# Top-k attention followed by an MLP: four units before the weight rounding, chunks from 128 tokens on, and one transpose for the leftover keys of both tiles

## The chip, the cores and the metric

The kernel runs on one core of a Trainium2 chip. The metric is device time in microseconds (us) of one execution, and the median over several executions is compared. Five engines with a queue of instructions each work side by side: TensorE (PE in the profile; its weight loads are PEld), VectorE (DVE), ScalarE (ACT), GpSimd (POOL) and SyncE (SP), which here only issues DMAs. Every engine takes its own instructions in the order in which the program issued them, and waits on semaphores for the others.

## The reference

Attention in which every query keeps its 32 best keys, for 8 batches of 8 heads with 576 tokens and 64 features per head, and then a two-layer MLP with a leaky ReLU on the 4608 tokens of 512 features (8 heads times 64):

```
scores = q @ k.T / sqrt(64)                     # per batch and head: 576 x 576
kth    = 32nd largest score of each row
scores = where(scores >= kth, scores, -1e9)
attn   = exp(scores - max) ; attn /= sum(attn) + 1e-9
x      = attn @ v                               # bridged to 4608 x 512
h      = x @ w_in                               # 512 x 2048
out    = max(0.01 * h, h) @ w_out               # 2048 x 512
```

The two weight matrices arrive as float64, everything else as float32; all matmuls run in float32.

## The kernel before, in words

**Units.** Heads are handled in pairs: 32 pairs, four per batch (HP = 4), and a pair's queries and keys lie in one 128-partition tile, head 0 on partitions 0 to 63, head 1 on 64 to 127. A *unit* is 256 rows of scores, held as two tiles of 128 rows x 576 keys (`u.s[0]`, `u.s[1]`). A whole unit is 128 queries of one pair, one head per tile. 576 = 4 x 128 + 64, so 64 queries per head are left over; a left unit takes these 64 queries of two pairs. There are 18 units per batch (16 whole, 2 left) and 144 in all. In even batches (`first`, line 161) the left units come first, in odd ones last, so that the left units of two neighbouring batches meet.

**Stages of a unit.** `scores` (L168): TensorE, and two ScalarE copies (L184) to SBUF. `top_k` (L187): VectorE, four rounds of "eight largest" (L194) on both tiles, with the eight found values struck out in between (L197). `mask` (L202): GpSimd, two passes per tile (L208, L210). `exponents` and `sums` (L212, L216): ScalarE. `reciprocals` (L220): one small VectorE instruction. `normalize` (L224): ScalarE. Then the normalized weights are transposed on TensorE with an identity as moving operand: the 576 keys are cut into five pieces (KLEN, L47), four of 115 keys and one of 116. `transpose_main` (L227) transposes the four pieces of one tile and copies them out (L234); `transpose_tail` (L236) transposes the fifth piece of each tile, two transposes, and copies both out (L240). `weigh_values` (L254) multiplies with the values (L262), ten matmuls per pair of heads, and ScalarE copies the result to the x tile of its chunk (L272).

**MLP.** The 4608 tokens are cut into chunks (CHUNKS, L51): 64, 128, 128, sixteen of 256 and one of 192. When all units of a chunk are through `weigh_values`, its MLP (`mlp`, L274) may start. It is a generator: 16 blocks of the first layer (L282, four matmuls each, then a leaky ReLU on ScalarE, L288) and, per 128 tokens, 16 matmuls of the second layer (L294). The chip executes each float32 matmul of these as two instructions, so a chunk has 128 instructions on L282 and 32 on L294 for each 128 tokens or part of them.

**Order of work.** Everything is issued by hand in steps (L397). In step s VectorE works on `top_k` of unit s, GpSimd on the mask of unit s-1, ScalarE on the exponents of unit s-2, and unit s-3 (LAG = 3, `oldest`) is normalized, transposed and weighed; `scores` of unit s+2 is issued near the end of the step, after `weigh_values`. In seven places (SLOTS) of a step `mlp_steps` issues a share of the MLP work that is ready, so that a chunk's MLP is spread evenly up to the step in which the next chunk becomes ready (`slot_budget`, L354). The last chunk's MLP comes after the loop (L446).

**Weight rounding.** The float64 weights come in 16 pieces of 1 MB, into three buffers (`raws`). `convert_weights` (L104) rounds a piece to float32: two VectorE passes (L112, L113), four ScalarE passes (L115 to L118), three more VectorE passes (L120 to L124). `convert` (L370) finishes the piece that was started two calls earlier, starts a new one, and issues the load of a later one. In the kernel before, units 0 and 1 (left units of batch 0) stand in steps 0 and 1; steps 2, 3 and 4 have no unit, and in each of them six calls of `convert` are issued (ROUNDED, L333), 18 calls for 16 pieces. Steps 5 on have units 2 on. Chunk 0 is ready after step 4, chunk 1 after step 11, chunk 2 after step 15, chunk 3 after step 23, and then a chunk every eight steps.

**Start.** The queries and keys of pairs 0 to 3, the scores of units 0 and 1 and the first weight pieces are issued ahead of the loop (L382 to L389).

Of the kernel before, what the change touches and what calls it, by code (L numbers as in the profile page):

```python
# [8 lines left out]
F32 = mybir.dt.float32  # L9
# [2 lines left out]
ALU = mybir.AluOpType  # L12

NKC = 5
KSTEP = 115


@with_exitstack
def kernel(
# [6 lines left out]
    moe_w_out: bass.AP,  # L26
    out: bass.AP,
):

    nc = tc.nc
    NPAIR, P, S = qT.shape
    D = P // 2
# [8 lines left out]
    HS = S // 2  # L43
    NFC = DFF // P
    ROUNDS = TOPK // 8
    WCH = 1024
    KLEN = [KSTEP] * (NKC - 1) + [S - (NKC - 1) * KSTEP]  # L47
    KMAX = KLEN[-1]
    LEFT = S % P
    assert D == 64 and S == 576 and HP == 4 and B % 2 == 0 and LEFT == 64  # L50
    CHUNKS = [64, 128, 128] + [256] * 16 + [192]  # L51
    assert sum(CHUNKS) == B * S
    CHMAX = max(CHUNKS)
    LOADED, LOADED_V = 6, 5
# [3 lines left out]
    loads = ctx.enter_context(tc.tile_pool(name="loads", bufs=LOADED))  # L58
    raws = ctx.enter_context(tc.tile_pool(name="raws", bufs=3))
    work = ctx.enter_context(tc.tile_pool(name="work", bufs=2))  # L60
    small = ctx.enter_context(tc.tile_pool(name="small", bufs=5))
    ps_sc = ctx.enter_context(tc.tile_pool(name="ps_sc", bufs=1, space=bass.MemoryType.PSUM))
    ps_tr = ctx.enter_context(tc.tile_pool(name="ps_tr", bufs=2, space=bass.MemoryType.PSUM))
    ps_ml = ctx.enter_context(tc.tile_pool(name="ps_ml", bufs=2, space=bass.MemoryType.PSUM))

    ident = const.tile([P, P], F32, name="ident")
# [61 lines left out]
    qk_of, v_of = {}, {}  # L128
# [6 lines left out]
        qk_of[pi] = qt, kt  # L135

    def load_v(pi):
        v_of[pi] = loads.tile([KMAX, NKC, 2, D], F32, name="vt", bufs=LOADED_V)
        nc.sync.dma_start(v_of[pi], vk[pi])

    class Unit:
# [3 lines left out]
        def __init__(self, b, pairs, q0):  # L145
            self.b, self.q0 = b, q0
            if len(pairs) == 1:
                self.rows = P
                self.parts = [(0, pairs[0], 0, 0), (1, pairs[0], 1, 0)]
                self.outs = [(pairs[0], 0, 1)]  # L150
            else:
                self.rows = LEFT

                self.parts = [(0, pairs[0], 0, 0), (1, pairs[0], 1, LEFT),
                              (1, pairs[1], 0, 0), (0, pairs[1], 1, LEFT)]
                self.outs = [(pairs[0], 0, 1), (pairs[1], 1, 0)]
            self.pairs = pairs

    units = []
    for b in range(B):  # L160
        first = b % 2 == 0
        whole = [Unit(b, [b * HP + hp], q0 + LEFT * first)
                 for q0 in range(0, S - LEFT, P) for hp in range(HP)]
        left = [Unit(b, [b * HP + hp, b * HP + hp + 1], 0 if first else S - LEFT)
                for hp in range(0, HP, 2)]
        units += left + whole if first else whole + left

    def scores(u):  # L168
        ps = [ps_sc.tile([P, 2, 512], F32, name=f"psc{i}") for i in range(2)]
        for n in range(0, len(u.parts), 2):  # L170
            for half in range(2):
                for i, pi, side, r0 in u.parts[n:n + 2]:
                    qt, kt = qk_of[pi]
                    d = slice(side * D, (side + 1) * D)
                    nc.tensor.matmul(  # L175
                        ps[i][r0:r0 + u.rows, half, 0:HS],
                        qt[d, u.q0:u.q0 + u.rows],
                        kt[d, half * HS:(half + 1) * HS],
                        start=True, stop=True,
                    )  # L180
        u.s = []
        for i in range(2):
            s_sb = work.tile([P, S], F32, name=f"s_sb{i}", bufs=5)
            nc.scalar.copy(s_sb.rearrange("p (h n) -> p h n", h=2), ps[i][:, :, 0:HS])  # L184
            u.s.append(s_sb)

    def top_k(u):  # L187

# [37 lines left out]

    def transpose_main(u, i):  # L227
        if i == 0:
            u.wT = work.tile([KMAX, 2, NKC, P], F32, name="wT")
        main = ps_tr.tile([P, 4, P], F32, name="main", tag="tr")  # L230
        for c in range(NKC - 1):
            nc.tensor.transpose(main[0:KLEN[c], c, :],  # L232
                                u.s[i][:, c * KSTEP:c * KSTEP + KLEN[c]], ident)
        nc.scalar.copy(u.wT[0:KSTEP, i, 0:NKC - 1, :], main[0:KSTEP])  # L234

    def transpose_tail(u):  # L236
        tail = ps_tr.tile([P, 2, P], F32, name="tail", tag="tr")
        for i in range(2):
            nc.tensor.transpose(tail[0:KMAX, i, :], u.s[i][:, (NKC - 1) * KSTEP:S], ident)  # L239
        nc.scalar.copy(u.wT[:, :, NKC - 1, :], tail[0:KMAX])  # L240

# [2 lines left out]
    def x_at(token):  # L246

        c = 0
        while token >= CHUNKS[c]:
            token -= CHUNKS[c]  # L250
            c += 1
        return c, token

    def weigh_values(u):  # L254
        n = u.rows
        po = ps_tr.tile([P, len(u.outs), n], F32, name="po", tag="tr")
        for o, (pi, i0, i1) in enumerate(u.outs):
            vt = v_of[pi]
            for c in range(NKC):
                for side, i in ((0, i0), (1, i1)):  # L260
                    r0 = LEFT * side if n < P else 0
                    nc.tensor.matmul(  # L262
                        po[side * D:(side + 1) * D, o, :],
                        vt[0:KLEN[c], c, side, :],
                        u.wT[0:KLEN[c], i, c, r0:r0 + n],
                        start=(c == 0), stop=(c == NKC - 1),
                    )
        ch, col = x_at(u.b * S + u.q0)
        if ch not in x_of:
            x_of[ch] = [xpool.tile([P, CHMAX], F32, name=f"x{c}") for c in range(HP)]  # L270
        for o, (pi, _, _) in enumerate(u.outs):
            nc.scalar.copy(x_of[ch][pi % HP][:, col:col + n], po[:, o, :])  # L272

    def mlp(ch):  # L274

        n = CHUNKS[ch]
        t0 = sum(CHUNKS[:ch])
# [32 lines left out]
    backlog, owed = [0.0], [0.0]  # L310
# [18 lines left out]
    LAG = 3  # L329


    steps = units[:2] + [None] * 3 + units[2:]
    ROUNDED = {2: 6, 3: 6, 4: 6}  # L333

    def unit(n):
        return steps[n] if 0 <= n < len(steps) else None
# [2 lines left out]
    for n, u in enumerate(steps):  # L339
        if u is None:  # L340
            continue
        ch, _ = x_at(u.b * S + u.q0)
# [11 lines left out]
    def slot_budget(s):  # L354

        after = [at for at, _ in ready_at if at >= s]
        return backlog[0] / ((after[0] + 1 - s if after else 1) * SLOTS)

    SLOTS = 7
    converting = []  # L360
# [3 lines left out]
    def fetch_weights():  # L364
        chunk = next(chunks, None)
        got = load_weights(*chunk) if chunk else None
        if got:
            raw_chunks.append(got)
# [11 lines left out]
    with tc.manual_schedule():  # L380
        last = {p: n for n, u in enumerate(steps) if u for p in u.pairs}
        for p in range(HP):  # L382
            load_qk(p)
            if p % 2:
                scores(units[p // 2])
                fetch_weights()
        for p in range(HP):
            load_v(p)
        fetch_weights()  # L389

        def load_more(s):

            for of, load, n, lag in ((qk_of, load_qk, LOADED, -2), (v_of, load_v, LOADED_V, LAG)):
                while len(of) < NPAIR and (len(of) < n or last[len(of) - n] + lag <= s):
                    load(len(of))

        for s in range(len(steps) + LAG):  # L397
            cur, old = unit(s), unit(s - 1)
            older, oldest, new = unit(s - 2), unit(s - LAG), unit(s + 2)
            picks = top_k(cur) if cur else iter(())  # L400
            budget = slot_budget(s)
            rounded = ROUNDED.get(s, 0)

            def slot(n):
                next(picks, None)
                for _ in range(rounded * n // 3 - rounded * (n - 1) // 3 if n else 0):
                    convert()

            slot(0)
            if old:  # L410
                mask(old, 0)
                mask(old, 1)
            if oldest:
                normalize(oldest, 0)
                normalize(oldest, 1)
            mlp_steps(budget)
            if older:
                exponents(older, 0)
            if oldest:
                transpose_main(oldest, 0)  # L420
            mlp_steps(budget)
            if older:
                exponents(older, 1)
                sums(older)
            slot(1)
            if oldest:
                transpose_main(oldest, 1)
            mlp_steps(budget)
            if oldest:
                transpose_tail(oldest)  # L430
            slot(2)
            mlp_steps(budget)
            if older:
                reciprocals(older)
            mlp_steps(budget)
            slot(3)
            if oldest:
                weigh_values(oldest)
            if new:
                scores(new)  # L440
            mlp_steps(budget)
            mlp_steps(budget)
            attended(s)
            if s >= max(ROUNDED):
                load_more(s)
        mlp_steps(1e9)  # L446

# [44 lines left out]
```

## Time and profile before

| | us |
|---|---|
| median of 3 runs (lowest to highest) | 1714.21 (1713.75 to 1714.6) |
| the profiled execution's own time | 1713.03 |
| its span in the profile | 1710.9 |
| TensorE busy (matmuls) | 1598.3 |
| VectorE busy | 1488.2 |
| GpSimd busy | 1079.5 |
| ScalarE busy | 1033.8 |

Busy time is the time in which an engine executes something; share and time alone do not say what a stage waits for. The chain that ended last is followed back from the last instruction and tells which engine's work stood in line. The span is shown in 40 slices of 42.8 us, with the busy share of each engine and the granted TensorE clock in tenths. "PE busy" counts matmuls that overlap in the pipeline; what a matmul costs in line is read from the distance between starts in the chain, not from the mean of one. L numbers are lines of the kernel before.

### The profile page before, as it was taken

The numbers are of one execution on the slowest core, as the hardware profiler recorded it, in microseconds if no ns is written. First come the engines' busy times: TensorE is split into PE (matmuls) and PEld (weight loads), VectorE is DVE, ScalarE is ACT, GpSimd is POOL, SyncE is SP. The second block draws the span as 40 slices with busy tenths as digits, with TensorE's granted clock in tenths as the row PEclk, the third lists the DMA queues.
The fourth block names the chain that finished last, engine by engine and source line by source line (L and its number), as shares of the span: only waits on it lengthen the run. The fifth ranks groups of instructions, "written<-read, shape, count | busy, mean of one in ns | idle before, by whom it ended". The sixth has DMA issues, their size and how long they took to land.

```text
span 1710.9 us, 26732 instructions
## 1 busy us (share of the span) xinstructions
PE 1598.3 (93%) x9664; PEld 1097.1 (64%) x9664; DVE 1488.2 (87%) x3106; ACT 1033.8 (60%) x2310; POOL 1079.5 (63%) x726
## 2 busy tenths in 40 slices
PE   1158998999999999999999999999999999999999
PEld 0146665858585858585758585858585858585764
DVE  7999999999899999999899999999899999999600
ACT  3965666656565656565656565656565656565530
POOL 4007777776667676767676767676667676767600
PEclk7557999999999999999999999999999999999999
DMA  5530010000110010000110010000100010000000
GB/s 181 197 133 1 5 62 23 14 7 9 61 35 7 7 62 28 14 8 7 63 35 7 7 62 28 14 7 7 63 35 7 7 35 28 7 7 7 7 13 10
DMA packets 21715, 56.30 MB, mean 33 GB/s; under 512 B 2000, under 2 KB 2000, under 8 KB 20560
## 3 DMA queue, kind: packets, MB, share of 16 engines
q1 hardware_dynamic: 21584, 54.60, 9.2%
q8 instruction: 77, 1.26, 0.3%
q14 instruction: 54, 0.44, 0.1%
HBM read 45.15 MB, written 9.44 MB: 32 GB/s over the span
## 4 chain that ended last, share of the span: by engine, by line
PE 85%; DVE 11%; ACT 3%; DMA 0%; issue 0%; SPq 0%; ACTq 0%
PE pz L294 29%; PE ph L282 28%; PE po L262 10%; PE psc L175 9%; PE main L232 7%; DVE tops L194 5%; DVE rest L197 4%; PE tail L239 2%; DVE ex L122 1%; ACT ex L116 1%; ACT ex L115 1%; DVE w_in L124 0%; ACT ex L117 0%; ACT s_sb L225 0%; ACT raw L118 0%; DVE w_in L120 0%
## 5 line engine op out<-in xcount | busy, mean ns | idle before, releaser
L208 POOL TENSOR_SCALAR pen<-s_sb,tops 128x576 f32<-128x576 f32 x288 | 638.0, 2215 | 417.7 <-ACT wT L240 214.0
L194 DVE MAX8 tops<-rest 128x8 f32<-128x576 f32 x864 | 608.1, 746 | 0.0
L282 PE MATMUL ph<-x,w_in 128*128 128x256 f32 (+3 forms) x2560 | 574.8, 369 | 4.3 <-ACT x L272 4.1
L294 PE MATMUL pz<-w_out,gT 128*128 128x512 f32 (+1 forms) x1184 | 553.7, 599 | 0.0
L282 PEld LDWEIGHTS ph<-x,w_in 128*128 128x128 f32 x2560 | 446.1, 196 | 82.8 <-issue 38.9
L197 DVE MATCH_REPLACE8 rest<-tops,rest 128x576 f32<-128x576 f32 x576 | 423.5, 743 | 0.0
L210 POOL TENSOR_TENSOR s_sb<-s_sb,pen 128x576 f32<-128x576 f32 x288 | 407.3, 1414 | 24.1
L294 PEld LDWEIGHTS pz<-w_out,gT 128*128 128x128 f32 (+1 forms) x1184 | 204.4, 187 | 203.5 <-issue 201.1
L232 PEld LDWEIGHTS main<-ident,s_sb 128*115 128x115 f32 x1152 | 165.3, 182 | 159.8 <-issue 92.2
L184 ACT COPY s_sb<-psc 128x576 f32<-128x576 f32 x288 | 170.0, 642 | 153.2 <-PE psc L175 153.2
L232 PE MATMUL main<-ident,s_sb 128*115 128x128 f32 x1152 | 177.8, 278 | 78.0 <-ACT s_sb L225 77.9
L213 ACT ACTIVATE s_sb<-s_sb,nbias 128x576 f32<-128x576 f32 x288 | 222.7, 773 | 10.9 <-POOL s_sb L210 10.9
L262 PEld LDWEIGHTS po<-wT,vt 115*64 115x64 f32 (+1 forms) x3200 | 160.0, 139 | 94.7 <-issue 73.8
L225 ACT ACTIVATE s_sb<-s_sb,rz 128x576 f32<-128x576 f32 x288 | 207.1, 770 | 9.9 <-DVE rz L222 9.7
L197 DVE MATCH_REPLACE8 rest<-tops,s_sb 128x576 f32<-128x576 f32 x288 | 211.7, 743 | 0.0
L262 PE MATMUL po<-wT,vt 115*64 115x128 f32 (+3 forms) x3200 | 193.6, 269 | 18.8 <-ACT wT L234 18.3
L194 DVE MAX8 tops<-s_sb 128x8 f32<-128x576 f32 x288 | 202.0, 743 | 9.5 <-ACT s_sb L184 9.5
L175 PE MATMUL psc<-kt,qt 64*128 64x288 f32 (+1 forms) x1280 | 202.5, 440 | 7.1 <-DMA kt<-in_kT_dram 7.1
L234 ACT COPY wT<-main 115x512 f32<-115x512 f32 x288 | 165.6, 575 | 58.5 <-PE main L232 58.3
L288 ACT ACTIVATE gT<-ph 128x256 f32<-128x256 f32 (+3 forms) x320 | 115.9, 363 | 135.8 <-PE ph L282 134.9
L272 ACT COPY x<-po 128x128 f32<-128x128 f32 (+1 forms) x160 | 39.3, 256 | 231.3 <-PE po L262 231.3
L175 PEld LDWEIGHTS psc<-kt,qt 64*128 64x128 f32 (+1 forms) x1280 | 108.7, 181 | 56.0 <-issue 23.4
(31 smaller groups left out, 535.3 us busy)
## 6 DMA issues: line engine op xcount, KB each, us to landing
vt<-in_vk_dram SPq DMA_DIRECT2D x32, 290.0 KB
qt<-in_qT_dram SPq DMA_DIRECT2D x32, 288.0 KB
kt<-in_kT_dram SPq DMA_DIRECT2D x32, 288.0 KB
out_dram<-o_sb SPq DMA_DIRECT2D x35, 256.0 KB
raw<-in_moe_w_in_dram SPq DMA_DIRECT2D x8, 1024.0 KB
raw<-in_moe_w_out_dram SPq DMA_DIRECT2D x8, 1024.0 KB
out_dram<-o_sb SPq DMA_DIRECT2D x2, 128.0 KB
```

What stands on the lines that cost most here:

```text
L175: nc.tensor.matmul(ps[i][r0:r0 + u.rows, half, 0:HS], qt[d, u.q0:u.q0 + u.rows], kt[d, half * HS:(half + 1) * HS], start=True, stop=True,)
L184: nc.scalar.copy(s_sb.rearrange("p (h n) -> p h n", h=2), ps[i][:, :, 0:HS])
L194: nc.vector.max(out=u.tops[:, i, r, :], in_=src[i])
L197: nc.vector.match_replace(out=rest[i], in_to_replace=u.tops[:, i, r, :], in_values=src[i], imm_value=LOWEST)
L208: nc.gpsimd.tensor_scalar(pen, u.s[i], u.tops[:, i, ROUNDS - 1, 7:8], MASKED, ALU.is_lt, ALU.mult)
L210: nc.gpsimd.tensor_tensor(u.s[i], u.s[i], pen, ALU.add)
L213: nc.scalar.activation(u.s[i], u.s[i], AF.Exp, bias=u.nbias[:, i:i + 1], scale=SCALE, accum_out=u.z[:, i:i + 1])
L225: nc.scalar.activation(u.s[i], u.s[i], AF.Copy, bias=0.0, scale=u.rz[:, i:i + 1])
L232: nc.tensor.transpose(main[0:KLEN[c], c, :], u.s[i][:, c * KSTEP:c * KSTEP + KLEN[c]], ident)
L262: nc.tensor.matmul(po[side * D:(side + 1) * D, o, :], vt[0:KLEN[c], c, side, :], u.wT[0:KLEN[c], i, c, r0:r0 + n], start=(c == 0), stop=(c ...
L282: nc.tensor.matmul(ph[:, 0:n], w_in[c][:, f * P:(f + 1) * P], x[c][:, 0:n], start=(c == 0), stop=(c == HP - 1),)
L294: nc.tensor.matmul(pz[0:m, 0:DMODEL], gT[f][:, r0:r0 + m], w_out[f // 4][:, f % 4, :], start=(f == 0), stop=(f == NFC - 1),)
```

## The change

Four things are changed together.

1. **Start and rounding.** The order of left and whole units is swapped between even and odd batches, so that batch 0 begins with whole units. Units 0 to 3 stand in steps 0 to 3. Steps 4 to 9 have no unit (`GAP = 6`), and in each of them three calls of `convert` are issued, 18 as before. Units 4 on stand in steps 10 on. In the steps without a unit, `scores` of a coming unit is issued at the start of the step instead of the end.
2. **Chunks.** 128, 128, then seventeen of 256. Units 0 to 3 are the first chunk; it is ready after step 6, and `slot_budget` spreads its MLP over steps 7 to 9. The second chunk (units at steps 10 to 13) is ready after step 16, the third after step 24, then one every eight steps. The chunk after the loop has 256 tokens instead of 192.
3. **Keys in pieces of 128.** The keys of head 1 are rotated by 64 places on the host. Four pieces of 128 keys per tile are transposed as before; head 0's 64 leftover keys are the last 64 columns of tile 0, and head 1's the first 64 columns of tile 1. The two score tiles become halves of one tile (`u.both`), so that these 128 columns lie side by side, and one transpose takes them both. The tail is one transpose and a copy of 128x128 instead of two and a copy of 116x256. The values are laid out by the host to match, with zeros for the other head's leftover keys.
4. **Left units** take head 0 in tile 0 and head 1 in tile 1 for both pairs.

```diff
-    CHUNKS = [64, 128, 128] + [256] * 16 + [192]
+    CHUNKS = [128] * 2 + [256] * 17
...
-        v_of[pi] = loads.tile([KMAX, NKC, 2, D], F32, name="vt", bufs=LOADED_V)
+        v_of[pi] = loads.tile([P, NKC, 2, D], F32, name="vt", bufs=LOADED_V)
...
-                self.outs = [(pairs[0], 0, 1)]
+                self.outs = [(pairs[0], 0, 0)]
...
-                              (1, pairs[1], 0, 0), (0, pairs[1], 1, LEFT)]
-                self.outs = [(pairs[0], 0, 1), (pairs[1], 1, 0)]
+                              (0, pairs[1], 0, LEFT), (1, pairs[1], 1, 0)]
+                self.outs = [(pairs[0], 0, LEFT), (pairs[1], LEFT, 0)]
...
-        first = b % 2 == 0
+        first = b % 2 == 1
...
-        u.s = []
+        u.both = work.tile([P, 2, S], F32, name="s_sb", bufs=5)
+        u.s = [u.both[:, i, :] for i in range(2)]
         for i in range(2):
-            s_sb = work.tile([P, S], F32, name=f"s_sb{i}", bufs=5)
-            nc.scalar.copy(s_sb.rearrange("p (h n) -> p h n", h=2), ps[i][:, :, 0:HS])
-            u.s.append(s_sb)
+            nc.scalar.copy(u.s[i].rearrange("p (h n) -> p h n", h=2), ps[i][:, :, 0:HS])
...
-            u.wT = work.tile([KMAX, 2, NKC, P], F32, name="wT")
+            u.wT = work.tile([P, 2 * (NKC - 1) + 1, P], F32, name="wT")
         main = ps_tr.tile([P, 4, P], F32, name="main", tag="tr")
         for c in range(NKC - 1):
-            nc.tensor.transpose(main[0:KLEN[c], c, :],
-                                u.s[i][:, c * KSTEP:c * KSTEP + KLEN[c]], ident)
-        nc.scalar.copy(u.wT[0:KSTEP, i, 0:NKC - 1, :], main[0:KSTEP])
+            k0 = c * P + i * (S - (NKC - 1) * P)
+            nc.tensor.transpose(main[:, c, :], u.s[i][:, k0:k0 + P], ident)
+        nc.scalar.copy(u.wT[:, i * (NKC - 1):(i + 1) * (NKC - 1), :], main)
 
     def transpose_tail(u):
-        tail = ps_tr.tile([P, 2, P], F32, name="tail", tag="tr")
-        for i in range(2):
-            nc.tensor.transpose(tail[0:KMAX, i, :], u.s[i][:, (NKC - 1) * KSTEP:S], ident)
-        nc.scalar.copy(u.wT[:, :, NKC - 1, :], tail[0:KMAX])
+        tail = ps_tr.tile([P, P], F32, name="tail", tag="tr")
+        both = u.both.rearrange("p i n -> p (i n)")
+        nc.tensor.transpose(tail, both[:, (NKC - 1) * P:NKC * P], ident)
+        nc.scalar.copy(u.wT[:, 2 * (NKC - 1), :], tail)
...
-                        vt[0:KLEN[c], c, side, :],
-                        u.wT[0:KLEN[c], i, c, r0:r0 + n],
+                        vt[:, c, side, :],
+                        u.wT[:, c + side * (NKC - 1) if c + 1 < NKC else 2 * (NKC - 1), r:r + n],
...
-    steps = units[:2] + [None] * 3 + units[2:]
-    ROUNDED = {2: 6, 3: 6, 4: 6}
+    FIRST, GAP = 4, 6
+    steps = units[:FIRST] + [None] * GAP + units[FIRST:]
+    gap = range(FIRST, FIRST + GAP)
...
         after = [at for at, _ in ready_at if at >= s]
-        return backlog[0] / ((after[0] + 1 - s if after else 1) * SLOTS)
+        until = gap[-1] if s in gap else after[0] if after else s
+        return backlog[0] / ((until + 1 - s) * SLOTS)
...
             load_qk(p)
-            if p % 2:
-                scores(units[p // 2])
-                fetch_weights()
+            if p < 2:
+                scores(units[p])
+        for _ in range(3):
+            fetch_weights()
         for p in range(HP):
             load_v(p)
-        fetch_weights()
...
-                for _ in range(rounded * n // 3 - rounded * (n - 1) // 3 if n else 0):
+                if s in gap and n:
                     convert()
 
             slot(0)
+            if new and s in gap:
+                scores(new)
...
-            if new:
+            if new and s not in gap:
                 scores(new)
...
-            if s >= max(ROUNDED):
+            if s >= gap[-1]:
                 load_more(s)
```

More of the change, by code (lines that the diff above doesn't have):

```diff
@@ L14 @@
 NKC = 5
-KSTEP = 115
 @with_exitstack
@@ L46 @@
     WCH = 1024
-    KLEN = [KSTEP] * (NKC - 1) + [S - (NKC - 1) * KSTEP]
-    KMAX = KLEN[-1]
     LEFT = S % P
     assert D == 64 and S == 576 and HP == 4 and B % 2 == 0 and LEFT == 64
-    CHUNKS = [64, 128, 128] + [256] * 16 + [192]
+    CHUNKS = [128] * 2 + [256] * 17
     assert sum(CHUNKS) == B * S
@@ L256, in weigh_values @@
         po = ps_tr.tile([P, len(u.outs), n], F32, name="po", tag="tr")
-        for o, (pi, i0, i1) in enumerate(u.outs):
+        for o, (pi, r0, r1) in enumerate(u.outs):
             vt = v_of[pi]
             for c in range(NKC):
-                for side, i in ((0, i0), (1, i1)):
-                    r0 = LEFT * side if n < P else 0
+                for side, r in ((0, r0), (1, r1)):
                     nc.tensor.matmul(
                         po[side * D:(side + 1) * D, o, :],
-                        vt[0:KLEN[c], c, side, :],
-                        u.wT[0:KLEN[c], i, c, r0:r0 + n],
+                        vt[:, c, side, :],
+                        u.wT[:, c + side * (NKC - 1) if c + 1 < NKC else 2 * (NKC - 1), r:r + n],
                         start=(c == 0), stop=(c == NKC - 1),
@@ L401 @@
             budget = slot_budget(s)
-            rounded = ROUNDED.get(s, 0)
             def slot(n):
                 next(picks, None)
-                for _ in range(rounded * n // 3 - rounded * (n - 1) // 3 if n else 0):
+                if s in gap and n:
                     convert()
             slot(0)
+            if new and s in gap:
+                scores(new)
             if old:
@@ L461, in by_pair, with keys_of_head_1_rotated @@
         return a.reshape(b * h // 2, 2, s, d).transpose(0, 1, 3, 2).reshape(b * h // 2, 2 * d, s)
+    def keys_of_head_1_rotated(a):
+        half = a.shape[1] // 2
+        return _np.concatenate([a[:, :half], _np.roll(a[:, half:], a.shape[2] % 128, axis=2)], axis=1)
     def by_key(a):
         b, h, s, d = a.shape
-        last = s - (NKC - 1) * KSTEP
-        keys = _np.arange(NKC)[None, :] * KSTEP + _np.arange(last)[:, None]
-        return a.reshape(b * h // 2, 2, s, d)[:, :, keys, :].transpose(0, 2, 3, 1, 4)
+        pairs, full, left = b * h // 2, s // 128, s % 128
+        a = a.reshape(pairs, 2, s, d)
+        laid = _np.zeros((pairs, 128, full + 1, 2, d), a.dtype)
+        laid[:, :, :full] = a[:, :, :full * 128].reshape(pairs, 2, full, 128, d).transpose(0, 3, 2, 1, 4)
+        for side in range(2):
+            laid[:, side * left:(side + 1) * left, full, side] = a[:, side, full * 128:]
+        return laid
     def bits(a):
@@ L473 @@
         "qT": by_pair(inputs["q"]),
-        "kT": by_pair(inputs["k"]),
+        "kT": keys_of_head_1_rotated(by_pair(inputs["k"])),
         "vk": by_key(inputs["v"]),
```

## The prediction

> **What bounds the kernel now.** I read the page first: engines, slices, chain by engine.
>
> ```profile
> PE 1598.3 (93%) x9664; PEld 1097.1 (64%) x9664; DVE 1488.2 (87%) x3106; ACT 1033.8 (60%) x2310; POOL 1079.5 (63%) x726
> ...
> PE   1158998999999999999999999999999999999999
> ...
> DVE  7999999999899999999899999999899999999600
> ...
> PEclk7557999999999999999999999999999999999999
> ...
> PE 85%; DVE 11%; ACT 3%; DMA 0%; issue 0%; SPq 0%; ACTq 0%
> ```
>
> TensorE is the chain from about slice 4 to the end; before that it idles at half clock and VectorE (later ScalarE) leads. So there are two sums: when the TensorE stretch begins, and how much TensorE work is left then. Next, the chain in order of time over the start:
>
> ```profile
> 10.40 1.41 DVE tops L194 x2
> ...
> 29.78 0.83 DVE ex L112
> ...
> 86.61 1.16 ACT ex L115
> ...
> 87.79 1.16 ACT ex L116
> ...
> 88.97 1.06 ACT ex L117
> 90.03 1.03 ACT raw L118
> ...
> 112.99 1.23 DVE w_out L120
> ...
> 116.60 1.32 DVE tops L194 x2
> ```
>
> Units 0 and 1 take 10.40 to 29.78, 9.69 us each. The rounding takes 86.8 us (29.8 to 116.6). ScalarE needs 4.38 us per weight piece (86.61 on; the neighbours 4.34 and 4.39), VectorE 4.86 (starts of L112 at 76.11 and 81.03, with a wait of 0.06): both are nearly full. After 116.6 a unit takes 9.70 us on VectorE while TensorE has little MLP; 19 steps and 2.1 us of waits later, at 302.9, step 24 brings the first 256-token MLP. From there steps take 10.6 us on TensorE:
>
> ```profile
> 571.63 0.44 PE main L232 x4
> ...
> 574.24 0.22 PE tail L239 x2
> 574.46 1.73 PE ph L282 x8
> 576.18 1.25 PE po L262 x20
> 577.43 1.17 PE psc L175 x8
> ...
> 1658.55 20.80 PE ph L282 x128
> 1679.35 27.62 PE pz L294 x64
> ```
>
> A transpose costs 0.11 us in line, a first-layer instruction of 256 columns 0.216 (1.73/8), one of 192 columns 0.1625 (20.80/128), a second-layer one 0.4315. The last two lines are the chunk after the loop. From 302.9 to the end of the span are 1408.0 us.
>
> **The change part by part.** The sum is against the profiled execution: 1713.03 us, span 1710.9; the median of 1714.21 is 1.2 above it and gets the same difference.
>
> *Start.* Unit 0 now needs pair 0 alone. Its inputs were there at 4.50 (first matmul on L175); eight instructions took 2.29 us at half clock (125.94), the copy 0.65: VectorE starts at 7.5 instead of 10.4. Four units of 9.69: rounding begins at 46.3. The swap of left and whole units costs nothing else here.
>
> *Rounding.* VectorE's work is the same 18 calls, 86.8 us if nothing else led. ScalarE gets more. Of units 1 to 3, what falls between the first and last piece: normalizations 1.33 per unit, exponents 1.75, copies of transposes 1.17, x 0.2; together 0.9 + 4.45 + 2.7. Sixteen leaky ReLUs of 128 columns (0.26 to 0.28 each): 4.2. Scores of units 4 and 5: 2 x 1.08. That is 14.4, with 16 x 4.38 = 70.1 in all 84.5; before it was 78.4 of busy time in the same stretch. ScalarE also waits for TensorE where several MLP shares lie between two pieces, since first-layer results have two buffers: two blocks at the start of step 7, scores and about three blocks between steps 7 and 8, a second-layer share and scores between 8 and 9. A block of eight 128-column instructions is 0.89 us at full clock (186.83 to 187.72) and, taken double, 1.78 at half. Counted along ScalarE's order, these waits are 6.9 us at full clock, 15.8 at half. TensorE is on and off there, so I take the middle, 11. With 0.94 ahead (first L112 to first L115), 3.6 behind (the last three VectorE passes) and 1.0 for waits on VectorE (3.9 before, when it led): 101 us, ending at 147.3. Ends: 89 (no such wait; VectorE's 86.8 lies below) and 107. That the MLP of chunk 0 itself is done by then costs nothing further: its TensorE time falls where TensorE was idle.
>
> *Steps 10 to 24.* Fifteen steps of 9.70 on VectorE: 145.5, ending at 292.8. Steps 10 to 16 have no MLP, and steps 17 to 24 spread 128 tokens over eight steps. That load is in the trace (steps 16 to 23, row 265.00), with VectorE full:
>
> ```profile
> 117.00:126.00 9.00, 9.00 (x41) 7.73 (x41) 9.00 (x20) 2.07 (x6) 0.44 (x2) 0.50 0.01 2
> 126.00:136.00 10.00, 10.00 (x45) 8.36 (x44) 10.00 (x22) 3.59 (x11) 7.83 (x6) 0.50 0.00 1
> ...
> 265.00:275.00 10.00, 7.54 (x67) 6.04 (x66) 10.00 (x22) 6.66 (x19) 7.78 (x6) 1.00 0.09 31
> ```
>
> (Windows; columns: length, busy PE, PEld, DVE, ACT, POOL, granted clock, DMA share, GB/s.) But there the clock was already full; now it will have fallen. In the rows at 117 and 126 TensorE was busy throughout and stayed at 0.50; it reached 1.00 at about 149, 4 us after transposes and MLP blocks began to alternate at 145.14. Step 17 alternates just so; 4 us at half clock lose about 2, part of it inside VectorE's cover: I take 1.5. Ends: 0, and 13 (a stretch like 117 to 140 at half clock, half of it lost).
>
> The Trainium skill, "TensorE: Matmul & The Clock Gate", Part 1, has full clock after some 3.4 us of sustained activity and half after an idle window of that length, and advises against idle gaps over 3 us, which steps 10 to 12 have. The 23 us at 0.50 disagree with the first half. By the page the loss would be 1.7 us, an estimate, and by the worse row 13.
>
> *TensorE work from there.* Before, at 302.9: 16 MLPs of 256 tokens and one of 192; 126 units to transpose and weigh, 121 to score. After, at 292.8: 17 of 256; 128 and 123. MLP: 128 x (0.216 - 0.1625) = +6.9; the second layer is the same 64 instructions per chunk, 192 or 256. Two units more: 2 x (0.88 + 1.25 + 1.17) = +6.6, less 1.8 since two fewer of the dearer left scores remain (2.09 against 1.17): +4.8. Tails: 126 x 0.22 against 128 x 0.11: -13.6. The main transposes' stationary tile grows from 115 to 128 columns: the nearest row is the first layer with 128 columns both ways, 0.111 per instruction against 0.11, +1.0. Ends: 0, and 8 x 128 x 14 ns = +14.3 if the whole difference of the mean loads (196 ns for 128 columns, 182 for 115) shows. Together -0.9. Ten weigh matmuls per pair of heads stay ten; a stationary tile of 64 columns stays 64.
>
> The same page (LDWEIGHTS) has the load grow with columns, P/1.2 ns, whatever the rows: 13 columns more are 10.8 ns, by estimate 11 us over the 1024 transposes if none is hidden. The 0.111 row speaks for hidden.
>
> *What hides the rest.* A TensorE step falls to 10.51 us; VectorE's 9.70 is next, 0.8 to spare, then GpSimd's 7.5 per unit. The smaller tail copy is off the path. SP: the values of pair 0 stand behind three weight pieces, 5.3 MB at 190 GB/s, about 28 us; they are needed near 45. A later piece's load had 7.3 us between its buffer's release (37.4) and its use (44.7) without a wait, and rounding gets slower. Later pairs are loaded from 147 instead of 117, and needed near 270.
>
> Sum: 292.8 - 302.9 = -10.1; +1.5; -0.9: -9.5. Profiled execution 1703.5, median 1704.7.
>
> **Rivals.**
> 1. Rounding stays as short as VectorE and ScalarE alone allow (89 us): 12 us less, 1692.7. For it: ScalarE waits hidden by MLP blocks done ahead during a piece. Against: two buffers.
> 2. Slower: the clock stays at half through steps 17 to 24. TensorE has 3.4 us of unit and 28.0/8 = 3.5 of MLP per step at full clock, 13.8 at half, against 9.70: 4.1 per step, 33 in all, 1736. It passes the old time from 2.7 such steps on. For it: 117 to 140 at 0.50; against: the rise at 149.
> 3. The loads of 128-column transposes show in full: +13.3, 1718, and the tail's gain is gone.
>
> **How the numbers follow.** My forecast 0.58 (of it 0.05 within 0.2%), rival 1 0.17, rival 2 0.10, rival 3 0.10 (half within 0.2%), others, such as steps above 9.70 or rounding beyond 107, 0.05, half of them slower. 0.2% (3.4 us) is about what a measurement can tell from no change. Faster 0.53 + 0.17 = 0.70; same 0.12; slower 0.18. Range 1692 (rival 1) to 1717 (the 13 us of cold clock, nearly all of rival 3); gap ends alone give 1693 to 1711. Rival 2 lies outside.
>
> **What would show it.** First L194 at 7.5; first L112 near 46, next L194 near 147 with ScalarE above 90% busy between; VectorE steps of 9.70 until 293; chain steps of 10.5; tail x1 at 0.11, main x4 still 0.44; a last chunk of 27.7 + 27.6. Wrong if the clock row reads 0.50 past step 17, if main x4 grows, or if the rounding misses 89 to 107.

## The result and the profile after

The changed kernel takes 1724.89 us (median of 4 runs, 1723.86 to 1725.7) against 1713.98 of the kernel before on the same chip: ratio 1.0065, 95% interval [1.0047, 1.0082]. It is slower by 11 us where 9.5 us less were forecast, and outside the range. The profiled execution took 1724.5 us, its span is 1722.3. Lines of the changed kernel have other numbers: L173 are the scores, L191 and L194 `top_k`, L222 `normalize`, L210 `exponents`, L230 and L236 the main and tail transposes, L258 `weigh_values`, L278 and L284 the first layer and its leaky ReLU, L290 the second layer, L113 to L116 ScalarE's part of the rounding.

The page of the changed kernel, engines, slices and chain by engine:

```profile
PE 1575.8 (91%) x9360; PEld 1057.2 (61%) x9360; DVE 1488.7 (86%) x3106; ACT 1014.5 (59%) x2293; POOL 1079.9 (63%) x726
...
PE   3255689999999999999999999999999999999999
...
PEclk9987589999999999999999999999999999999999
...
PE 80%; DVE 10%; ACT 9%; issue 0%; DMA 0%; SPq 0%; ACTq 0%
```

TensorE is busy 22 us less, as the change removes transposes and matmuls, but it is on the chain for 80% instead of 85% of the span, and ScalarE's share rose from 3% to 9%. Part of that is the rounding. The 9s with which the clock row begins are not to be taken at their word: the eight score instructions at 4.45 took 2.31 us, where eight later ones take 1.17. The chain in order of time over the start:

```profile
4.45 2.31 PE psc L173 x8
...
7.41 1.41 DVE tops L191 x2
...
43.35 1.46 DVE rest L194 x2
...
142.61 1.23 DVE w_out L118
...
146.23 1.32 DVE tops L191 x2
...
280.66 1.44 ACT s_sb L222 x2
...
291.19 0.66 PE main L230 x4
```

VectorE starts at 7.41; the last two searches of unit 3 end near 46.1; the rounding lasts to 146.23; VectorE leads until 280.5, and the first transposes of step 25, with which the first 256-token MLP begins, start at 291.19. In the kernel before they belong to step 24:

```profile
302.47 0.69 PE L232 MATMUL main<-ident,s_sb 128*115 128x128 f32 x4 [0.35 <-ACT s_sb L225]
```

So the start brought 11.3 us. They were lost afterwards: from there to the end of the span are 1431.1 us, before 1408.4. The chain in the middle of the run, over one step with first-layer work:

```profile
557.91 1.94 PE ph L278 x8
559.85 0.02 issue
559.87 0.38 ACT gT L284
560.25 0.67 ACT s_sb L222
560.92 0.04 issue
560.97 0.66 PE main L230 x4
561.63 0.86 PE ph L278 x4
562.49 0.44 PE main L230 x4
...
563.79 0.11 PE tail L236
...
568.91 1.94 PE ph L278 x8
```

The step takes 11.00 us (557.91 to 568.91), 0.38 more than before in spite of the cheaper tail. The chain leaves TensorE after eight instructions of the first layer: ScalarE applies the leaky ReLU to the block that has just ended (0.38), then normalizes tile 0 of the next unit (0.67), and only then the transposes of that tile may start. Meanwhile TensorE has one more share of MLP work, four instructions, 0.86 us; then it stands still for 0.28 us. In the kernel before, sixteen first-layer instructions stood ahead of the first transposes, and no ScalarE line was on the chain.

A step without the wait takes 10.51 us (first experiment below), so the wait costs 0.49, more than the 0.28. The timeline of another such step shows the rest. In it the transposes of tile 0 wait, those of tile 1 do not; the number in brackets is the idle time before, with what ended it:

```profile
647.08 0.42 PEld L230 LDWEIGHTS main<-ident,s_sb 128*128 128x128 f32 x4 [0.68 <-ACT s_sb L222]
647.08 0.66 PE L230 MATMUL main<-ident,s_sb 128*128 128x128 f32 x4 [0.28 <-ACT s_sb L222]
...
647.57 1.03 PE L278 MATMUL ph<-x,w_in 128*128 128x256 f32 x4
...
648.23 0.57 PEld L230 LDWEIGHTS main<-ident,s_sb 128*128 128x128 f32 x4
...
648.44 0.60 PE L230 MATMUL main<-ident,s_sb 128*128 128x128 f32 x4
...
648.88 1.03 PE L278 MATMUL ph<-x,w_in 128*128 128x256 f32 x4
```

The chain's 0.66 and 0.44 for `main` are not the same measure. After a wait the chain counts from the first start to the last end; without one it counts from the end of the matmul before, which is still running when the first transpose starts. From start to start the four transposes take 0.49 after the wait (647.08 to 647.57) and 0.44 without (648.44 to 648.88). These 0.05 us go with the first weight load, which begins together with the first transpose after the wait (both 647.08), and 0.21 ahead of it without one (648.23). The remaining 0.16 are lost overlap: a first-layer instruction lasts 0.38, and where nothing waits the next one starts 0.22 after it. (Starts are recorded; the ends of matmuls, and so the 0.28 and the 0.16, are modelled by the profiler. By starts alone the step loses 0.44 ahead of the transposes and 0.05 in them.)

In the steps with second-layer work there is no such wait, but at the end of a chunk the copy of the result (L297, 0.59) stands ahead of the normalization in the same way: that step takes 11.18 us (from 630.45 to 641.63, between two pieces of L258 in the chain), against 10.48 in the first experiment. The idle time in the long stretch, by windows (length, busy PE, PEld, DVE, ACT, POOL, clock, DMA share, GB/s):

```profile
565.00:650.00 85.00, 83.69 (x500) 55.23 (x500) 77.49 (x166) 51.33 (x120) 59.92 (x40) 1.00 0.10 35
```

TensorE was busy throughout in this window before:

```profile
565.00:650.00 85.00, 85.00 (x499) 58.46 (x497) 78.59 (x170) 53.22 (x122) 60.05 (x41) 1.00 0.11 35
```

### The profile page after: what moved, and what is told of

Read it like the earlier page. It is cut to its first block, busy times and chain, and to the rows that moved or that the text cites. A ratio compares the mean times of both kernels' runs of the same rounds, so it can differ in the third digit from the quotient of the medians.

```text
span 1722.3 us, 25823 instructions
## 1 busy us (share of the span) xinstructions
PE 1575.8 (91%) x9360; PEld 1057.2 (61%) x9360; DVE 1488.7 (86%) x3106; ACT 1014.5 (59%) x2293; POOL 1079.9 (63%) x726
## 4 chain that ended last, share of the span: by engine, by line
PE 80%; DVE 10%; ACT 9%; issue 0%; DMA 0%; SPq 0%; ACTq 0%
PE pz L290 28%; PE ph L278 25%; PE po L258 9%; PE psc L173 9%; PE main L230 7%; DVE tops L191 5%; DVE rest L194 5%; ACT s_sb L222 3%; ACT gT L284 1%; ACT ex L114 1%; ACT ex L115 1%; ACT ex L113 1%; ACT raw L116 1%; PE tail L236 1%; ACT o_sb L297 1%
## 5 line engine op out<-in xcount | busy, mean ns | idle before, releaser
L191 DVE MAX8 tops<-rest 128x8 f32<-128x576 f32 x864 | 608.3, 746 | 0.0
L278 PE MATMUL ph<-x,w_in 128*128 128x256 f32 (+1 forms) x2432 | 562.9, 378 | 15.8 <-ACT gT L284 10.8
L290 PE MATMUL pz<-w_out,gT 128*128 128x512 f32 x1152 | 535.8, 600 | 0.9 <-ACT gT L284 0.9
L278 PEld LDWEIGHTS ph<-x,w_in 128*128 128x128 f32 x2432 | 434.2, 196 | 99.9 <-issue 35.7
L194 DVE MATCH_REPLACE8 rest<-tops,rest 128x576 f32<-128x576 f32 x576 | 423.6, 744 | 0.0
L290 PEld LDWEIGHTS pz<-w_out,gT 128*128 128x128 f32 x1152 | 203.4, 190 | 217.9 <-issue 215.4
L230 PE MATMUL main<-ident,s_sb 128*128 128x128 f32 x1152 | 175.1, 287 | 96.6 <-ACT s_sb L222 96.6
L230 PEld LDWEIGHTS main<-ident,s_sb 128*128 128x128 f32 x1152 | 138.6, 146 | 173.0 <-ACT s_sb L222 121.4
L210 ACT ACTIVATE s_sb<-s_sb,nbias 128x576 f32<-128x576 f32 x288 | 222.0, 771 | 14.8 <-POOL s_sb L207 14.8
L258 PEld LDWEIGHTS po<-wT,vt 128*64 128x64 f32 x3200 | 164.8, 141 | 96.9 <-issue 70.9
L222 ACT ACTIVATE s_sb<-s_sb,rz 128x576 f32<-128x576 f32 x288 | 207.3, 771 | 28.0 <-DVE rz L219 28.0
L258 PE MATMUL po<-wT,vt 128*64 128x128 f32 (+1 forms) x3200 | 199.1, 275 | 21.7 <-ACT wT L231 21.7
L194 DVE MATCH_REPLACE8 rest<-tops,s_sb 128x576 f32<-128x576 f32 x288 | 211.8, 744 | 0.0
L284 ACT ACTIVATE gT<-ph 128x256 f32<-128x256 f32 (+1 forms) x304 | 113.2, 374 | 166.0 <-PE ph L278 160.9
L191 DVE MAX8 tops<-s_sb 128x8 f32<-128x576 f32 x288 | 202.2, 744 | 6.5 <-ACT s_sb L182 6.5
L173 PE MATMUL psc<-kt,qt 64*128 64x288 f32 (+1 forms) x1280 | 188.6, 439 | 6.5 <-DMA kt<-in_kT_dram 4.4
L231 ACT COPY wT<-main 128x512 f32<-128x512 f32 x288 | 164.2, 570 | 28.7 <-PE main L230 28.7
L219 DVE RECIPROCAL rz<-ze 128x2 f32<-128x2 f32 x144 | 23.7, 165 | 133.3 <-ACT ze L215 133.3
```

The source lines that it names most:

```text
L173: nc.tensor.matmul(ps[i][r0:r0 + u.rows, half, 0:HS], qt[d, u.q0:u.q0 + u.rows], kt[d, half * HS:(half + 1) * HS], start=True, stop=True,)
L191: nc.vector.max(out=u.tops[:, i, r, :], in_=src[i])
L194: nc.vector.match_replace(out=rest[i], in_to_replace=u.tops[:, i, r, :], in_values=src[i], imm_value=LOWEST)
L210: nc.scalar.activation(u.s[i], u.s[i], AF.Exp, bias=u.nbias[:, i:i + 1], scale=SCALE, accum_out=u.z[:, i:i + 1])
L222: nc.scalar.activation(u.s[i], u.s[i], AF.Copy, bias=0.0, scale=u.rz[:, i:i + 1])
L230: nc.tensor.transpose(main[:, c, :], u.s[i][:, k0:k0 + P], ident)
```

## Where the shares of a chunk fall

Why there are four instructions ahead of the transposes and not eight can be read from the code. In each of seven slots of a step `mlp_steps` adds a budget to a debt and issues shares until the debt is paid. For a chunk of 256 tokens the budget is 32768 / 56 = 585 and a share of the first layer (half a block, four instructions) costs 512, so a step issues eight shares in seven slots, and one slot gets two. Which one depends on the debt that is carried in, and since 56 budgets pay a chunk exactly, that debt is the same at the start of every chunk. Worked through, it is -6.1 in the kernel before and -326.7 in the changed one, left over from the short chunks of the start. With `h` for the first half of a block and `H` for the second:

```
slot                     1    2    3    4    5    6    7
before   (debt -6.1)     hH   h    H    h    H    h    H
changed  (debt -326.7)   h    H    h    H    hH   h    H
```

Scores stand ahead of slot 6. The normalization is issued after slot 7, the first transposes between slots 1 and 2. In both kernels a block ends in slot 7, and its leaky ReLU is issued just ahead of the normalization. What TensorE has to do in the meantime is slot 1: 1.73 us before, 0.86 us now, against 0.38 + 0.67 + 0.04 = 1.1 us on ScalarE.

That gives theory A: the whole loss is this wait, 3 x 0.50 us in the first-layer steps plus 0.69 at the chunk's end, 2.2 us in each of 16 chunks, 35 us. Theory B: transposes with a stationary tile of 128 columns load too slowly, for which the chain's 0.66 for `main` could also be taken (rival 3 of the prediction). Theory C: TensorE's clock suffers from the longer start (rival 2).

## The experiments

**The changed kernel with the old debt.**

```diff
             budget = slot_budget(s)
+            if s == 25:
+                owed[0] = -6.1
```

> The changed kernel, but with the MLP's debt set to -6.1 at step 25, the value that the kernel before carries, so that the slot that issues two MLP shares is the first of a step instead of the fifth; all instructions are the same, in another order. Theory A (the lost time is the wait of the first transposes for the normalization, because only one share of 0.86 us lies between the end of a first-layer block and them): the wait goes from the four steps of each 256-token chunk, which costs 3 x 0.50 + 0.69 = 2.2 us in each of 16 chunks, 35 us; the time is about 1690, steps of 10.5 throughout. Theory B (stationary tiles of 128 columns load too slowly, so main x4 takes 0.66 where it took 0.44): the same loads are made, so 1717 to 1725. Theory C (TensorE's clock after the longer start): unchanged, 1725.

Measured 1688.15 us, ratio to before 0.9851 [0.9836, 0.9866]. Its chain at the same place:

```profile
560.89 3.65 PE ph L278 x16
564.54 0.44 PE main L230 x4
...
571.40 3.65 PE ph L278 x16
```

Sixteen instructions, then transposes at 0.44, steps of 10.51. One number in the schedule is worth 36.7 us. Theories B and C fall: stationary tiles of 128 columns and the long start are still there.

**The kernel before with the debt of the changed one.**

```diff
             budget = slot_budget(s)
+            if s == 24:
+                owed[0] = -326.7
```

> The kernel before, with the MLP's debt set to -326.7 at step 24, the value that the changed kernel carries, so that the fifth slot of a step issues two shares instead of the first. Theory A: the wait appears with the old keys and the old start too: about 2.2 us in each of 15 to 16 chunks, 1714 + 33 to 35, about 1748, ScalarE's normalization on the chain and first-layer steps of about 11.1 us. Theories B and C: nothing that they blame is in this kernel, so 1714.

Measured 1751.2, ratio 1.0218 [1.0203, 1.0233]; 37.7 us slower than before:

```profile
577.76 1.94 PE ph L282 x8
...
579.72 0.38 ACT gT L288
580.11 0.67 ACT s_sb L225
...
580.82 0.69 PE main L232 x4
...
588.91 1.94 PE ph L282 x8
```

The wait appears with old keys and old start, steps take 11.15, and the chain has 0.69 for `main` with 115 columns too. So this figure goes with the wait, not with the 128 columns.

**The two halves of the change apart.** First the keys, the tail and the left units on the schedule of before, then the schedule on the keys and left units of before. The edit of the first, cut to its main lines, against the changed kernel:

```diff
-    CHUNKS = [128] * 2 + [256] * 17
+    CHUNKS = [64, 128, 128] + [256] * 16 + [192]
...
-        first = b % 2 == 1
+        first = b % 2 == 0
...
-    FIRST, GAP = 4, 6
-    steps = units[:FIRST] + [None] * GAP + units[FIRST:]
+    steps = units[:2] + [None] * 3 + units[2:]
+    ROUNDED = {2: 6, 3: 6, 4: 6}
```

> The keys in pieces of 128, one tail transpose and the new left units, with the start, the chunks and the order of batches of the kernel before. Theory A: the debt is -6.1 as before, so no wait; 126 tails less (13.9 us) and 14 left scores at 1.14 instead of 2.09 (13 us): about 1687. Theory B: the loads of 128 columns show here too, 8 x 126 of 11 to 14 ns or 0.22 per wait, so 1698 to 1714. Theory C: 1687, as A.

Measured 1684.89, ratio 0.9831 [0.9814, 0.9847].

> The start with four units, the six short rounding steps, the chunks and the order of batches of the changed kernel, with keys in pieces of 115 and two tail transposes as before. Theory A: the debt is -326.7, so the wait is there: 11 us gained at the start, 12 more of TensorE work left then (64 columns in the last chunk, two units), 35 of waits: about 1749. Theory B: 1714 to 1716, since the loads are of 115 columns. Theory C: 1714 plus the loss to the clock, about 1740, but with the lost time before 400 us and not in every chunk.

Measured 1753.97, ratio 1.0234 [1.0219, 1.025]. The keys, the tail and the left units give 29 us, the schedule takes 40; together 11.8, and the changed kernel measured 10.9 above before: the parts add up. Of the schedule's 40 us, 36.7 are the wait (changed kernel against the first experiment). The rest is seen between the first and the third experiment, which have the same keys and the same debt: 3.3 us in the medians, 2.3 in the profiled executions. In their traces the first layer of the first 256-token chunk begins at 289.8 with the new schedule and at 300.6 with the old one, and from there to the end are 1396.2 and 1383.1 us: 10.8 gained at the start, 13.1 more work left then. By the rows of the prediction it is 13.5 (6.9 for the last chunk, 6.6 for two units).

**The pairing of the left units alone.** In the kernel before, the second pair puts head 0 into tile 1:

```diff
-                              (1, pairs[1], 0, 0), (0, pairs[1], 1, LEFT)]
+                              (0, pairs[1], 0, LEFT), (1, pairs[1], 1, 0)]
```

(with the matching rows in `weigh_values`).

> The kernel before with one edit: the second pair of a left unit puts head 0 in tile 0 and head 1 in tile 1, so that its two scores go to the other two quarters of the array. In the changed kernel such 16 instructions took 1.14 us in line, before 2.09. If the pairing alone does this: 14 left units after step 24 at 0.95, 13 us less, about 1701. If it came from something else in the change (the rotated keys, the joined tile): 1714.

Measured 1701.4, ratio 0.9933 [0.9918, 0.9948]: 12.3 us. The scores of a left unit, first in this kernel, then in the kernel before:

```profile
808.97 1.14 PE psc L175 x16
```

```profile
810.54 2.09 PE psc L175 x16
```

**The normalization a step earlier.** The debt of the changed kernel is kept; `normalize` of a unit is issued ahead of `weigh_values` of the step before its transposes.

```diff
-            if oldest:
-                normalize(oldest, 0)
-                normalize(oldest, 1)
             mlp_steps(budget)
...
             slot(3)
+            if older:
+                normalize(older, 0)
+                normalize(older, 1)
             if oldest:
                 weigh_values(oldest)
```

> The changed kernel with the debt left as it is, but a unit's normalization issued at the end of the step before, ahead of weigh_values, instead of at the start of the step in which it is transposed. Theory A (the transposes wait for a normalization that stands behind a leaky ReLU on ScalarE): the wait goes whatever the debt, about 1690. If the wait is not for the normalization but for something else at that place (buffers of the transposes, the loads): 1717 to 1725.

Measured 1689.83, ratio 0.9863 [0.9847, 0.988]. The shares fall as in the changed kernel, but nothing waits:

```profile
562.89 2.79 PE ph L278 x12
565.68 0.44 PE main L230 x4
...
573.40 2.79 PE ph L278 x12
```

> Both of the edits that should take the wait away, the debt of -6.1 at step 25 and the normalization issued a step earlier. Theory A: they remove the same wait, so together no better than either alone: 1688 to 1691. If each removes a different wait, it is faster than the better of the two by more than 5 us.

Measured 1690.46, ratio 0.9865 [0.9851, 0.988]: no better than either alone. Both edits remove the same wait.

**Two shares in the sixth slot.** The debt is -402: `h H h H h Hh H`. Four shares stand between scores and transposes, as before, but slot 1 still has one.

> The changed kernel with the MLP's debt set to -402 at step 25: the sixth slot issues two shares. Between the scores and the first transposes lie then four shares, as many as in the kernel before, but the block of the first layer that ends last before the normalization still ends in slot 7, with one share after it. Theory A1 (what counts is the work left to TensorE between the end of that block and the transposes, 0.86 us against 1.1 of ScalarE): the wait stays, about 1723. Theory A2 (what counts is how many shares stand between scores and transposes): the wait goes, about 1689.

Measured 1725.32, ratio 1.0063 [1.0048, 1.0078]:

```profile
569.90 2.80 PE ph L278 x12
...
572.73 0.39 ACT gT L284
573.12 0.67 ACT s_sb L222
...
573.83 0.66 PE main L230 x4
```

The number of shares ahead of the transposes is not what counts. It is the work left to TensorE after the end of the last block whose leaky ReLU stands ahead of the normalization.

**Chunks of 128 throughout.** An attempt at a better version, with the normalization early so that the debt plays no part:

```diff
-    CHUNKS = [128] * 2 + [256] * 17
+    CHUNKS = [128] * 36
```

> The changed kernel with the normalization a step early and all 36 chunks of 128 tokens, so that the MLP of a chunk is spread over four steps from step 17 on and TensorE no longer waits through steps 17 to 24. If TensorE's work bounds from the step at which it is full: 8 steps x (9.7 - 6.9) = 22 us gained, and 17 x 0.7 = 12 lost, since two first-layer instructions of 128 columns take 0.222 and one of 256 takes 0.216: about 1680. If small chunks bring waits of their own (two blocks of 0.89 us per share, leaky ReLUs twice as many): 1690 to 1710.

Measured 1708.3, ratio 0.9967 [0.9954, 0.9979].

> The keys and left units of the changed kernel on the start of the kernel before (two units, three rounding steps), with the normalization a step early and chunks of 64, thirty-five times 128, and 64. By the same sums as for the short chunks on the new start: the start with two units has VectorE at 116.6 instead of 146.2 with two units less done, 10 us behind, but starts its MLPs of 128 tokens two steps earlier; about 1680, within 5 of the other. If short chunks bring waits of their own: 1690 to 1710.

Measured 1712.55, ratio 0.999 [0.9981, 0.9999]. Both miss 1680 by about 30 us. In the first of the two the chain passes through ScalarE at the end of every chunk, that is every four steps:

```profile
603.68 0.59 ACT o_sb L297
604.26 0.77 ACT s_sb L210 x2
...
607.38 1.16 PE ph L278 x8
...
646.44 0.59 ACT o_sb L297
```

Four steps take 42.76 us, 10.69 each, where the chunks of 256 with early normalization have 10.51 (562.89 to 573.40 above). So short chunks bring a wait of their own, again behind ScalarE's in-order queue. Over units 40 to 140 VectorE's first searches lie 10.76 us apart on average, against 10.49 in the sixth experiment: 0.27 a step more, where the expectation had 12 us in all for short chunks, under 0.1 a step. That no other term was wrong is not shown.

The fastest version measured is the new keys and left units on the old start and chunks: 1684.89 us, 1.7% below the kernel before. Its interval overlaps that of the first experiment (1688.15).

## Why the prediction was wrong

**The start: right.** Forecast against trace: first search 7.5, 7.41; rounding from 46.3, about 46.1; its end 147.3, 146.23; VectorE's first search of step 25 at 292.8, 291.55. The rounding took 100.1 us against 101. In it ScalarE was busy for 84.2 (84.5 were worked out), and its waits for TensorE add up to 10.8 (idle time before its instructions from 48.5 to 142.5). The 11 set aside for these was a choice between 6.9 and 15.8, not a derivation, so that it fits so closely is in part luck. The sign "ScalarE above 90% busy" did not come: it was 84%, which is also what the prediction's own 84.5 of 101 give. Rival 1 (89 us of rounding) falls.

**Steps 10 to 24, the clock: right that it costs little.** The clock was at half for long, in the rows from 160 to 200, and VectorE stayed full. From 215 on, where steps 17 to 24 lie, rows of 5 us read between 0.62 and 1.00. Windows of the changed kernel:

```profile
190.00:195.00 5.00, 3.06 (x16) 1.63 (x13) 5.00 (x11) 2.54 (x5) 2.96 (x4) 0.50 0.00 0
...
245.00:250.00 5.00, 5.00 (x40) 4.53 (x42) 5.00 (x13) 2.12 (x7) 4.82 (x3) 0.62 0.02 3
```

The fifteen steps took 145.3 us (146.23 to 291.55) where 145.5 were forecast. The 1.5 us set aside for the clock were not needed; rival 2 falls.

**TensorE's work from there: two terms wrong.** Forecast 1407.1 us after VectorE's first search of step 25 (the prediction's 302.9 and 292.8 are such searches), measured 1430.8. The step that failed is "A TensorE step falls to 10.51 us; VectorE's 9.70 is next". It took the order of TensorE's work around the transposes as given and only made one instruction cheaper, and among what could come next it names VectorE and GpSimd, not the order in which ScalarE serves the transposes. 10.51 is exactly what the steps take once the shares fall as before (first experiment); with the debt of the changed kernel the first-layer steps took 11.00. The forecast counted the work of the new chunk list but did not ask in which slot the shares come, although the profile of before showed what the slot covers: sixteen first-layer instructions, then `main` at 0.44 with no ScalarE on the chain. Worth +35 by the chain's lines (16 x 2.2), 36.7 by the runs. None of the rivals had it.

The second term has the other sign. "less 1.8 since two fewer of the dearer left scores remain (2.09 against 1.17)" priced the left units as before; the new pairing made them cheap. Twelve left units in that stretch at 2.09 - 1.14 give -11.4. Together 35.0 - 11.4 = +23.6, against the 23.7 that were missing. The Trainium skill, "TensorEngine Tiling (Array Packing)", Tiling Modes, lists four independent tiles of 64x64, and would have pointed to it: before, the second pair's two matmuls used the same two quarters of the array as the first pair's, now they use the other two. The 1.14 against 2.09 agrees.

**Transposes: right in the price, wrong on the load.** The tail is one transpose of 0.11, `main` of 128 columns takes 0.44 where it does not wait (first experiment), so rival 3 falls. Its price came from a row of other matmuls: 196 ns for the first layer's loads of 128 columns against 182 for the transposes' loads of 115. The transposes' own loads became shorter, with 128 columns first and with 115 second (shortest, median and longest in ns):

```profile
L230 PEld LDWEIGHTS main<-ident,s_sb x968: 137/141/146, 302.3 to 1597.0; 128*128 128x128 f32 x194
```

```profile
L232 PEld LDWEIGHTS main<-ident,s_sb x952: 175/179/179, 313.0 to 1577.9; 128*115 128x115 f32 x191
```

The Trainium skill has weight loads grow with the columns ("TensorE: Matmul & The Clock Gate", LDWEIGHTS); these rows disagree, and what makes the load of 128 columns shorter is not shown. The tail's gain is seen between the third and the fifth experiment, which differ in the keys. From the first layer of the first 256-token chunk to the end the profiled executions have 1383.1 and 1397.2 us: 14.1 less, where 13.9 were worked out. The new keys gained another 2.1 us ahead of that point (300.6 against 302.7), which was not followed.

**The last chunk** took 27.6 + 27.5 where 27.7 + 27.6 were forecast:

```profile
1663.43 27.63 PE ph L278 x128
1691.05 27.48 PE pz L290 x64
```

So the sum was nearly right on what was counted, the left scores apart, and the time went to an order of instructions that the diff changes only through a remainder.

## What to carry to other kernels

Where work is interleaved by a budget with a running remainder, any change of sizes at the start moves that remainder, and with it the place of every later share: compare the order of instructions around each wait in the steady stretch, not only the counts. For every instruction that waits, add up what the releasing engine must still do in order (here a ReLU and a normalization, 1.1 us), and what the waiting engine has left to do meanwhile (0.86 or 1.73 us). Issuing the released work a stage earlier removed such a wait here without touching the remainder (sixth experiment, 1689.83 us), and setting the remainder alone did as much (first experiment, 1688.15).

## What the runs showed of the hardware that was not expected

- A wait of TensorE cost more than its idle time: 0.28 us of standing still made the step 0.49 longer. About 0.16 of it is overlap of neighbouring matmuls that a wait does away with, 0.05 the first weight load that was not done ahead.
- The weight load of a transpose took 141 ns with 128 columns and 179 with 115.
- The sixteen score instructions of a left unit took 1.14 us where they used all four quarters of the array, and 2.09 where they used two.
- TensorE at half clock for most of steps 11 to 16 (rows from 160 to 200) cost nothing, as VectorE's 9.70 us per step covered it.
